# Attention into two feed-forward layers on one core: written order for the first two blocks, weight signs on ScalarE, integer sums on VectorE

## The chip, the cores and the metric

The kernel runs on one core of one Trainium2 chip. The metric is the device time of the program in microseconds (us). Five engines run side by side, each through its own queue of instructions in order: TensorE (PE in the profile; PEld is its weight load), VectorE (DVE), ScalarE (ACT), GpSimd (POOL) and SyncE (SP), which here only issues transfers. They meet at semaphores.

## What is computed

```python
q_d, k_d, v_d = means of q, k, v over groups of 4 positions   # 4 batches, 8 heads, 576 positions, width 64
out_up    = repeat(softmax(q_d k_d' / 8) v_d, 4)              # 144 pooled positions
out_local = softmax(q k' / 8, |i - j| < 4 only) v             # a band of 7 positions
x = (out_up + out_local) as 2304 x 512
y = (x w_a) * (x w_b) @ w_out                                 # 512 -> 1536 -> 512
h = y @ w_in                                                  # 512 -> 1024
s = h * softmax(h); s = (s - mean) / sqrt(var + 1e-6) * g
out = s @ w_out2                                              # 1024 -> 512
```

All inputs are 32-bit floats, except that the two layers' weights arrive as 64-bit floats, two 32-bit words each, and are made into 32-bit floats on the chip.

## The kernel before

The 2304 rows of x are cut into 18 tiles of 128 rows (s = 0 to 17), and two tiles make a block of 256 (0 to 8). Every matrix product on the long path is done three times in a reduced 32-bit format: the operand's high part by the weight's high part, the low part by the high, the high part by the low.

**Attention.** For each batch, `pooled_items` works on four pairs of heads (hp): VectorE sums q and k over 4 positions into `qkds` (L175), TensorE makes scores `S` (L196), VectorE their maximum (L206), ScalarE the exponentials `E` (L212), VectorE and GpSimd the normalisation (L218 to L221), TensorE turns `E` (`PT`, L232) and multiplies by the v that GpSimd has summed (`vds`, L184 and L185; `pv`, L244), and ScalarE writes `up`. `local_items` does the band for a tile s: scores `lS`, mask and maximum (L324 to L328), exponential, sum and normalisation (L335 to L338), turn (`lPT`), product with v (`lo`), the sum with `up` (L373) and the split into high and low part, `xTh` and `xTl` (L380, L381).

**Weights.** `w_stages` makes one 128 x 512 weight tile: transfer `raw` (L91), two ScalarE passes over the high and the low words (L99, L100), on VectorE a shift (L104) and the sign put back (L105), an integer sum of the two words on GpSimd (L110), the high part on ScalarE (L116) and the low part on VectorE (L123). There are 36 tiles for the first layer (three for each of 12 chunks j) and 16 for the second.

**First layer.** `emit_A` makes the two products of one block and one chunk (`ab`, 24 matmuls, L399) and multiplies them (L404 to L411); `emit_B` adds the third product (`acc` or `accS`, 12 matmuls, L426). A unit of A and B is called a step here; there are 108, and B comes two steps behind A. The list `subs` sets their order: three steps of block 0, then blocks 1 and 0 in turn, then one block after the other. A second phase (`emit_C`, `emit_chain`, `emit_D`) does the second layer, tile by tile.

**Order.** Attention and weight work is put on a list with places in units of half a step (`add(t, f)`) and called as the steps go by (`advance`). A scheduler then orders the instructions of each engine by its own timeline; before, `issue_after` held a few ScalarE instructions back in it (L82, L98).

Of the kernel before, what the change touches and what calls it, by code (L numbers as in the profile page):

```python
# [18 lines left out]
NP = H // 2  # L19
# [10 lines left out]
LEAD = 3  # L30
PT = [0, 16, 17]

# [6 lines left out]
def kernel(  # L39
# [17 lines left out]
    PE, ACT, DVE, POOL = nc.tensor, nc.scalar, nc.vector, nc.gpsimd  # L57
# [8 lines left out]
    mk_sb = base.tile([128, 4, KW], F32, name="mk_sb")  # L66
# [11 lines left out]
    gate = []  # L78

    def behind():  # L80

        return tc.issue_after(gate[-1].ins) if gate else nullcontext()  # L82

    def w_stages(src, i, dst, at, gcol=None, lo_eng=DVE):
# [4 lines left out]
        def load():  # L89
            raw = slot(at, I32, (128, 1024), "raw")  # L90
            nc.sync.dma_start(out=raw, in_=src[i])  # L91
            words = raw.rearrange("p (a b) -> p a b", b=2)
            st["low"], st["high"] = words[:, :, 0], words[:, :, 1]

        def s1():
            hw = f32(st["high"])
            prev = his.get((id(dst), i - 4))
            with behind(), (tc.issue_after(prev.ins) if prev else nullcontext()):  # L98
                ACT.activation(out=hw, in_=hw, func=AF.Copy, scale=2.0 ** -112)  # L99
                ACT.activation(out=st["low"], in_=st["low"].bitcast(U32), func=AF.Copy, scale=2.0 ** -29)  # L100

        def s2():
            st["w"] = base.tile([128, 512], I32, tag="wm", bufs=3, name="wm")
            DVE.tensor_scalar(out=st["w"], in0=st["high"], scalar1=3, scalar2=None, op0=ALU.logical_shift_left)  # L104
            DVE.scalar_tensor_tensor(  # L105
                out=st["w"], in0=st["high"], scalar=-(2 ** 31), in1=st["w"], op0=ALU.bitwise_and, op1=ALU.bitwise_or
            )

        def s3():
            POOL.tensor_tensor(out=st["w"], in0=st["w"], in1=st["low"], op=ALU.add)  # L110

        def s4():
            t = slot(at)
            dst[i] = t[:, 0, :], t[:, 1, :]
            if gcol is None:
                his[id(dst), i] = ACT.copy(out=dst[i][0], in_=f32(st["w"]))  # L116
            else:
                his[id(dst), i] = ACT.activation(out=dst[i][0], in_=f32(st["w"]), func=AF.Copy, scale=gcol)
# [12 lines left out]
    his = {}  # L131
# [20 lines left out]
    def load_qkr(i):  # L152
# [6 lines left out]
        for n in range(2):  # L159
            nc.sync.dma_start(out=qkr[i][n], in_=qkp[i, :, n, :])  # L160

    def load_v(i):
        t = slot(32 + i, F32, (128, 2, 512), "vp")[:72] if i < NP else pool_p.tile([72, 2, 512], F32, tag="vp", name="vp")
        nc.sync.dma_start(out=t, in_=vp[i])
        vr[i] = t

    def pooled_items(b, hp):
        i = b * NP + hp
        st = {}

# [17 lines left out]
        def scores():  # L188
            if b:
                st["S"] = [aps.tile([72, 2 * SD], F32, tag=f"x{e}", name="S") for e in range(2)]  # L190
            else:
                t = aps.tile([72, 2, 512], F32, tag="S", name="S")
                st["S"] = [t[:, e, 0:2 * SD] for e in range(2)]
            for half in range(2):
# [7 lines left out]
        def smax():  # L202
# [5 lines left out]
            st["E"] = pool_p.tile([72, 2, 2, SD], F32, tag="E", name="E")  # L208
# [31 lines left out]
        def pvm():  # L240
            st["pv"] = aps.tile([128, SD], F32, tag="x0", name="pv")
            for kh in range(2):
                for e in range(2):
                    PE.matmul(  # L244
                        out=st["pv"][e * 64:e * 64 + 64, :],
                        lhsT=st["v"][:, kh, e * 64:e * 64 + 64],
                        rhs=st["PTs"][:, e, kh, :], start=(kh == 0), stop=(kh == 1))
# [6 lines left out]
        items = [(0, qsum(0)), (0.5, qsum(1)), (1.5, scores), (2, vsum(0)), (2.2, vsum(1)),  # L254
                 (2.5, smax), (4.5, norm), (6, ptr), (7, pte), (8, pvm), (9, pve)]
        if b:
            items = [(-3, lambda: load_qkr(i)), (-2.9, lambda: load_v(i))] + items
        return items

    def load_local(s, st):  # L260
# [487 lines left out]
```

## Time and profile before

| | |
|---|---|
| median of 3 runs | 870.78 us (868.38 to 873.15) |
| profiled execution | 875.02 us, its span 871.6 us |
| TensorE busy | 803.8 us, 92% of the span |
| VectorE / ScalarE / GpSimd busy | 47% / 39% / 40% |
| mean granted TensorE clock | 0.988 of full speed |

The profile is of one execution. A row of a timeline gives the start, the duration, the engine, the line and the tiles (result <- operands), the number of instructions merged into it, and in brackets the idle time ahead of it and who ended it. A busy TensorE in such rows includes matmuls at its lower clock.

### The profile page before, as it was taken

The page shows a single profiled execution, that of the slowest core. Times are in us where ns is not written, and L with a number is a line of the kernel's source. Part 1 is how long each engine was busy: PE and PEld are TensorE (multiplying, and loading weights), DVE is VectorE, ACT ScalarE, POOL GpSimd, SP SyncE. Part 2 cuts the span into 40 slices and gives each one's busy share as a digit, 9 for nine tenths or more (in the row PEclk, how much of TensorE's full clock was granted, in tenths as well). Part 3 has the DMA queues.
Part 4 walks back from the last instruction along what each step waited for, and adds up shares of the span by engine and source line. Part 5 has one row for each costly group of instructions (what it writes and reads, how often), then busy time and mean ns, then how long its engine had stood idle before and what let it go on. Part 6 is the DMA issues. An engine that isn't in the chain of part 4 may idle for free. (4 is left out here: it accounts for less than half of the span.)

```text
span 871.6 us, 15806 instructions
## 1 busy us (share of the span) xinstructions
PE 803.8 (92%) x6456; PEld 731.6 (84%) x6456; DVE 411.8 (47%) x720; ACT 342.6 (39%) x768; POOL 351.3 (40%) x335
## 2 busy tenths in 40 slices
PE   2248898989999999999999999999989999999997
PEld 2137887979999999999999999999888888888886
DVE  4797689982223232223232221222894825555542
ACT  1654466752333333223332222323753534343432
POOL 2675576763133333223322222222883334333320
PEclk9999799999999999999999999999999999999999
DMA  7998300121212222112111110003730544444420
GB/s 203 339 300 316 116 14 29 42 66 53 82 49 77 66 66 66 53 41 73 44 40 40 49 39 15 25 8 102 258 101 25 157 145 141 142 142 145 132 73 36
DMA packets 65655, 85.21 MB, mean 98 GB/s; under 512 B 9368, under 2 KB 46552, under 8 KB 65584
## 3 DMA queue, kind: packets, MB, share of 16 engines
q1 hardware_dynamic: 55792, 79.49, 29.2%
q10 hardware_dynamic: 9792, 4.72, 1.9%
q8 instruction: 50, 0.82, 0.4%
q14 instruction: 21, 0.17, 0.1%
HBM read 66.89 MB, written 17.30 MB: 97 GB/s over the span
## 5 line engine op out<-in xcount | busy, mean ns | idle before, releaser
L399 PE MATMUL ab<-xTh,w 128*128 128x256 f32 x1728 | 348.0, 290 | 9.0 <-DVE a L407 7.5
L399 PEld LDWEIGHTS ab<-xTh,w 128*128 128x128 f32 x1728 | 282.9, 194 | 17.2 <-DVE a L407 9.2
L399 PE MATMUL ab<-xTl,w 128*128 128x256 f32 x864 | 247.2, 286 | 0.0
L411 POOL TENSOR_TENSOR pl<-a,ph 128x256 fp32r<-128x256 f32 x108 | 88.5, 820 | 210.0 <-ACT ph L410 210.0
L399 PEld LDWEIGHTS ab<-xTl,w 128*128 128x128 f32 x864 | 167.5, 194 | 1.0 <-issue 0.8
L407 DVE TENSOR_TENSOR a<-a,ab 128x256 f32<-128x256 f32 x108 | 45.0, 416 | 211.8 <-ACT a L404 211.7
L467 PE MATMUL h<-w,o1w 128*128 128x512 f32 x432 | 102.9, 391 | 1.3 <-DVE ss L491 1.3
L404 ACT COPY a<-ab 128x256 f32<-128x256 f32 x108 | 40.1, 371 | 157.2 <-PE ab L399 145.6
L426 PE MATMUL acc<-ph,w 128*128 128x256 f32 x480 | 98.4, 286 | 1.6 <-ACT ph L410 1.6
L110 POOL TENSOR_TENSOR wm<-wm,raw 128x512 int32<-128x512 int32 x52 | 79.9, 1542 | 40.9 <-DVE wm L105 22.1
L467 PEld LDWEIGHTS h<-w,o1w 128*128 128x128 f32 x432 | 80.5, 188 | 18.7 <-ACT o1w L455 1.7
L535 PE MATMUL o<-w,cTh 128*128 128x512 f32 x288 | 90.9, 397 | 0.9 <-ACT cTh L525 0.9
L426 PEld LDWEIGHTS acc<-ph,w 128*128 128x128 f32 x480 | 80.2, 194 | 2.5 <-ACT ph L410 1.8
L426 PE MATMUL accS<-ph,w 128*128 128x256 f32 x384 | 80.4, 290 | 0.0
L426 PE MATMUL acc<-pl,w 128*128 128x256 f32 x240 | 68.8, 288 | 0.5 <-POOL pl L411 0.5
L535 PEld LDWEIGHTS o<-w,cTh 128*128 128x128 f32 x288 | 54.1, 188 | 13.8 <-ACT cTh L525 1.1
L426 PEld LDWEIGHTS accS<-ph,w 128*128 128x128 f32 x384 | 64.8, 196 | 0.9 <-issue 0.6
L410 ACT CAST ph<-a 128x256 fp32r<-128x256 f32 x108 | 43.8, 405 | 38.1 <-DVE a L407 37.9
L535 PE MATMUL o<-w,cTl 128*128 128x512 f32 x144 | 57.2, 397 | 0.1
L519 POOL TENSOR_TENSOR cTl<-raw,cTh 128x1024 fp32r<-128x1024 f32 x15 | 36.0, 2402 | 50.4 <-ACT cTh L518 50.3
L426 PE MATMUL accS<-pl,w 128*128 128x256 f32 x192 | 55.4, 288 | 0.4 <-POOL pl L411 0.4
L105 DVE SCALAR_TENSOR_TENSOR wm<-raw,wm 128x512 int32<-128x512 int32 x52 | 50.9, 989 | 1.1
(84 smaller groups left out, 1118.8 us busy)
## 6 DMA issues: line engine op xcount, KB each, us to landing
raw<-w SPq DMA_DIRECT2D x52, 512.0 KB
qkr<-qkp SPq DMA_DIRECT2D x32, 288.0 KB
vd<-v SPq DMA_DIRECT2D x15, 512.0 KB
raw<-vd SPq DMA_DIRECT2D x60, 128.0 KB
vw<-vwin SPq DMA_DIRECT2D x36, 140.0 KB
vp<-vp SPq DMA_DIRECT2D x16, 288.0 KB
o1d<-o ACTq DMA_DIRECT2D x36, 128.0 KB
o1r<-o1d SPq DMA_DIRECT2D x18, 256.0 KB
```

Of the source, the lines that this page charges most:

```text
L105: DVE.scalar_tensor_tensor(out=st["w"], in0=st["high"], scalar=-(2 ** 31), in1=st["w"], op0=ALU.bitwise_and, op1=ALU.bitwise_or)
L110: POOL.tensor_tensor(out=st["w"], in0=st["w"], in1=st["low"], op=ALU.add)
L399: PE.matmul(out=ab[:, n, :], lhsT=w[:, ws], rhs=x[:, k, :], start=(k == 0 and i == 0), stop=(k == 3 and i == 2), skip_group_check=True)
L404: g_ = ACT.copy(out=a, in_=ab[:, 0, :])
L407: DVE.tensor_tensor(out=a, in0=a, in1=ab[:, 1, :], op=ALU.mult)
L410: ACT.copy(out=ph, in_=a)
L411: POOL.tensor_tensor(out=pl, in0=a, in1=f32(ph), op=ALU.subtract)
L426: PE.matmul(out=accs[blk][m // 2][:, m % 2, :], lhsT=w[:, ms], rhs=x, start=(j == 0 and i == 0 and m % 2 == 0), stop=(j == NCH - 1 and i = ...
L467: PE.matmul(out=h[:, n * 512:n * 512 + 512], lhsT=x[:, ks], rhs=w, start=(k == 0 and q_ == 0), stop=(k == 3 and q_ == 2))
L519: POOL.tensor_tensor(out=h4(lo), in0=raw, in1=f32(h4(hi)), op=ALU.subtract)
L535: PE.matmul(out=o, lhsT=x[:, k, :], rhs=w, start=(k == 0 and q_ == 0), stop=(k == 7 and q_ == 2))
```

## The change

- q and k of batch 0 are fetched first; mask and identity go to ScalarE's transfer queue, and an exponential of one column loads ScalarE's table at the start.
- For batch 0, v is no longer summed on GpSimd: TensorE multiplies by each of the four parts (16 matmuls for a pair of heads in place of 4).
- The sign is kept by a two-sided slope (`Prelu`) in the ScalarE pass over the high words, so L105 goes; the integer sum moves from GpSimd to VectorE.
- `LEAD` is 1: blocks 0 and 1 take turns from the first step, so all four tiles s = 0 to 3 are finished ahead of the first step.
- `pin` ties each instruction to the one written before it on its engine, for all that is written up to step 24; the early part has a new table of places. The three `issue_after` holds are gone.
- Twelve first-layer tiles (20 before) are fetched ahead; the buffer `o1` is single; scratch of the early part moves to slots of later weights (12 to 19).

```diff
-LEAD = 3
+LEAD = 1
+STRICT = 24
...
+    def pin():
+        traced = nc.cur_bb.bb.instructions
+        for ins in traced[done[0]:]:
+            if ins.engine in last:
+                tc.add_manual_dep(
+                    ins, last[ins.engine].name,
+                    mybir.DependencyInfo(mybir.DependencyClass.NoSync, mybir.DependencyReason.DATA), reason="pin")
+            last[ins.engine] = ins
...
-            with behind(), (tc.issue_after(prev.ins) if prev else nullcontext()):
-                ACT.activation(out=hw, in_=hw, func=AF.Copy, scale=2.0 ** -112)
+            ACT.activation(out=hw, in_=hw, func=AF.Prelu, scale=2.0 ** -112, alpha=2.0 ** 32)
...
-            DVE.scalar_tensor_tensor(
-                out=st["w"], in0=st["high"], scalar=-(2 ** 31), in1=st["w"], op0=ALU.bitwise_and, op1=ALU.bitwise_or
-            )
...
-            POOL.tensor_tensor(out=st["w"], in0=st["w"], in1=st["low"], op=ALU.add)
+            DVE.tensor_tensor(out=st["w"], in0=st["w"], in1=st["low"], op=ALU.add)
...
+                v = [vr[i][:, kh, 2 * D * t:2 * D * t + 2 * D] for kh in range(2) for t in range(4)]
...
+            if s < 4:
+                x = slot(16 + s, F32, (128, NP, 256), "lx")[:, :, 0:128]
...
-                o1 = base.tile([128, 2, 256], F32, tag="o1", bufs=2, name="o1")
+                o1 = base.tile([128, 2, 256], F32, tag="o1", name="o1")
...
+    for hp, ts in enumerate(((4.8, 5.5, 6.3, 7.6, 8.5, 10.7, 12, 13.9, 14.5, 18.4),
...
-        t = (-20, -14, -8)[j] + 0.8 * (i % 3) if j < LEAD else w_due[j] - 8 + 0.8 * (i % 3)
+        t = 4 * j - 6 + 1.33 * (i % 3)
...
+    ACT.dma_start(out=mk_sb[0:64, :], in_=band)
+    ACT.dma_start(out=mk_sb[64:128, 0:4], in_=band[:, 1:5])
+    ACT.dma_start(out=id_sb, in_=ident)
+    warm = base.tile([128, 1], F32, name="warm")
+    ACT.activation(out=warm, in_=mhalf, func=AF.Exp)
...
+        if u <= STRICT:
+            pin()
```

TensorE, the last attention work ahead of the first step, before: `ab` is the first step's tile, `lS` 16 times is a further tile's scores.

```order
L232 MATMUL PT<-id_sb,E 72x72 x8
L348 MATMUL lPT<-id_sb,lP 70x128 x4
L244 MATMUL pv<-PTs,vds 64x144 x4
L348 MATMUL lPT<-id_sb,lP 70x128 x8
L361 MATMUL lo<-lPTs,vw 64x64 x8
L348 MATMUL lPT<-id_sb,lP 70x128 x4
L361 MATMUL lo<-lPTs,vw 64x64 x24
L399 MATMUL ab<-xTh,w_485 128x256
L399 MATMUL ab<-xTh,w_512 128x256
L317 MATMUL lS<-qkr 64x70 x16
```

The same place now, from the last pair of heads' `pv` on.

```order
L269 MATMUL pv<-PTs,vp 64x144 x16
L394 MATMUL lo<-lPTs,vw 64x64 x16
L375 MATMUL lPT<-id_sb,lP 70x128 x8
L394 MATMUL lo<-lPTs,vw 64x64 x16
L375 MATMUL lPT<-id_sb,lP 70x128 x8
L394 MATMUL lo<-lPTs,vw 64x64 x16
L439 MATMUL ab<-xTh,w_508 128x256
L439 MATMUL ab<-xTl,w_508 128x256
```

Tiles 2 and 3 (the last two pairs of `lPT` and `lo`) now stand ahead of the first `ab`, and a `pv` has 16 matmuls.

SyncE's queue behind the first transfers, before: `raw` is a weight tile, `vw` the band's v; the last two rows are batch 1's first q, k and v.

```order
L91 DMA raw<-w 128x1024 x3
L271 DMA vw<-vwin 70x512 x4
L91 DMA raw<-w 128x1024 x18
L160 DMA qkr<-qkp 128x576 x2
L164 DMA vp<-vp 72x1024
```

The same place now; the seven `raw` of the third row are weight tiles 13 to 19.

```order
L100 DMA raw<-w 128x1024 x10
L703 DMA g_sb<-g 128x8
L100 DMA raw<-w 128x1024 x7
L606 DMA mk_sb<-band 64x70
L165 DMA qkr<-qkp 128x576 x2
L169 DMA vp<-vp 72x1024
```

Batch 1's q and k still stand behind the weights, and the last four of these weights (16 to 19) now go into slots that hold the sums `lx` of tiles 0 to 3.

VectorE where the first step's end meets the next weights, now (the second `qkds` rows are batch 1's, `w_674` and `w_703` are tiles 3 and 4).

```order
L410 TENSOR_TENSOR lx<-lo,up 128x4x128
L113 TENSOR_SCALAR wm<-raw 128x512
L116 ISA wm<-raw,wm 128x1024
L186 TENSOR_REDUCE qkds<-qkr 128x144
L113 TENSOR_SCALAR wm<-raw 128x512
L116 ISA wm<-raw,wm 128x1024
L186 TENSOR_REDUCE qkds<-qkr 128x144
L129 TENSOR_TENSOR w_674<-wm,w_674 128x512
L445 TENSOR_TENSOR a<-a,ab 128x256
L113 TENSOR_SCALAR wm<-raw 128x512
L116 ISA wm<-raw,wm 128x1024
L129 TENSOR_TENSOR w_703<-wm,w_703 128x512
```

The integer sum (L116) is there an instruction over 1024 elements, and the low parts of tiles 3 and 4 stand behind both sums of batch 1.

## Rows read from the trace of the kernel before

**Rows 1.** Busy time by stretch: five engines, granted clock, transfer share, GB/s.
```profile
0.00:75.90 75.90, 30.27 (x273) 21.08 (x273) 52.28 (x82) 34.25 (x86) 42.25 (x42) 1.00 0.88 278
75.90:234.10 158.20, 147.01 (x1267) 137.66 (x1268) 113.04 (x161) 80.02 (x190) 91.85 (x82) 0.95 0.23 75
234.10:600.00 365.90, 365.90 (x3573) 351.71 (x3572) 98.59 (x221) 107.72 (x287) 104.85 (x128) 1.00 0.17 49
```
**Rows 2.** Timeline, the end of the start: TensorE from 65 us on.
```profile
65.29 1.34 PE L244 MATMUL pv<-PTs,vds 72*64 72x144 f32 x8 [0.85 <-POOL vds L185]
66.56 1.92 PE L348 MATMUL lPT<-id_sb,lP 128*70 128x128 f32 x8
...
72.48 1.98 PE L361 MATMUL lo<-lPTs,vw 70*64 70x64 f32 x32 [0.86 <-DVE lx L373]
75.90 0.80 PE L399 MATMUL ab<-xTh,w 128*128 128x256 f32 x2 [1.44 <-ACT xTh L380]
```
**Rows 3.** One line, ScalarE L432: start of the first and the last.
```profile
L432 ACT COPY o<-accS x8: 566/588/592, 234.1 to 611.8; 128x512 f32<-128x512 f32 x8
```
**Rows 4.** TensorE's waits, 0 to 75.9 us: total, times, longest.
```profile
PE PT L232 <- POOL E L221: 17.2, 4, 5.4
PE lS L317 <- DMA qkr<-qkp: 12.3, 3, 8.9
```
**Rows 5.** Timeline, the first transfers and matmuls.
```profile
0.74 0.39 SPq L624 DMA_DIRECT2D id_sb<-ident  x1
...
4.95 3.75 SPq L160 DMA_DIRECT2D qkr<-qkp  x8
...
8.92 0.51 PE L317 MATMUL lS<-qkr 64*64 64x70 f32 x8 [8.92 <-DMA qkr<-qkp]
...
9.71 1.24 PE L196 MATMUL S<-qkds 64*72 64x144 f32 x8 [0.28 <-DVE qkds L175]
```
**Rows 6.** VectorE by line and shape, 0 to 234.1 us.
```profile
L123 DVE TENSOR_TENSOR w<-wm,w 128x512 fp32r<-128x512 f32 x36 | 43.6, 1227 | 4.5 <-ACT w L116 4.5
L105 DVE SCALAR_TENSOR_TENSOR wm<-raw,wm 128x512 int32<-128x512 int32 x36 | 35.1, 983 | 0.8
L104 DVE TENSOR_SCALAR wm<-raw 128x512 int32<-128x512 int32 x36 | 27.5, 770 | 6.8 <-ACT raw L99 6.5
L175 DVE TENSOR_REDUCE qkds<-qkr 128x144 f32<-128x576 f32 x18 | 12.7, 740 | 7.3 <-DMA qkr<-qkp 7.3
...
L373 DVE TENSOR_TENSOR lx<-lo,up 128x512 f32<-128x512 f32 x5 | 3.5, 690 | 3.5 <-PE lo L361 3.5
```
**Rows 7.** Timeline, VectorE and GpSimd on weights.
```profile
26.72 0.43 DVE L104 TENSOR_SCALAR wm<-raw 128x512 int32<-128x512 int32 x1 [4.91 <-ACT raw L99]
...
31.20 3.03 POOL L110 TENSOR_TENSOR wm<-wm,raw 128x512 int32<-128x512 int32 x2 [6.28 <-DVE wm L105]
31.59 1.50 DVE L104 TENSOR_SCALAR wm<-raw 128x512 int32<-128x512 int32 x1
...
34.91 0.68 DVE L105 SCALAR_TENSOR_TENSOR wm<-raw,wm 128x512 int32<-128x512 int32 x1
```
**Rows 8.** VectorE by line and shape, 640 us to the end.
```profile
L480 DVE SCALAR_TENSOR_TENSOR u<-h,u 128x1024 f32<-128x1024 f32 x18 | 22.1, 1225 | 36.1 <-ACT u L479 36.1
```
**Rows 9.** The chain that ended last: start, duration, what.
```profile
662.35 2.88 PE acc L426 x24
```
**Rows 10.** TensorE by line, 75.9 to 234.1 us: first and last of seven attention groups.
```profile
L196 PE MATMUL S<-qkds 64*72 64x144 f32 x32 | 6.7, 338 | 0.4 <-ACT up L252 0.4
...
L317 PE MATMUL lS<-qkr 64*64 64x70 f32 x32 | 1.2, 327 | 0.0
```
**Rows 11.** ScalarE by line and shape, 0 to 234.1 us.
```profile
L99 ACT ACTIVATE raw<-raw 128x512 f32<-128x512 f32 x36 | 24.4, 679 | 9.2 <-DMA raw<-w 9.2
...
L116 ACT CAST w<-wm 128x512 fp32r<-128x512 f32 x36 | 22.3, 620 | 33.6 <-POOL wm L110 33.5
```
**Rows 12.** TensorE's waits, 600 to 672 us.
```profile
PE ab L399 <- DVE a L407: 4.9, 3, 2.6
```

More of the change, by code (lines that the diff above doesn't have):

```diff
@@ L1 @@
-from contextlib import ExitStack, nullcontext
+from contextlib import ExitStack
 import concourse.bass as bass
@@ L241, in pvm @@
             st["pv"] = aps.tile([128, SD], F32, tag="x0", name="pv")
-            for kh in range(2):
+            if b:
+                v = [st["v"][:, kh] for kh in range(2)]
+            else:
+                v = [vr[i][:, kh, 2 * D * t:2 * D * t + 2 * D] for kh in range(2) for t in range(4)]
+            for n, vt in enumerate(v):
                 for e in range(2):
[L244 to L247, printed above, removed]
+                    PE.matmul(out=st["pv"][e * 64:e * 64 + 64, :], lhsT=vt[:, e * 64:e * 64 + 64],
+                              rhs=st["PTs"][:, e, n * 2 // len(v), :], start=(n == 0), stop=(n == len(v) - 1))
         def pve():
@@ L575 @@
-    first += [f for _, f in locs[1][1][:2]]
-    for a, b in zip(locs[0][1][2:], locs[1][1][2:]):
-        first += [a[1], b[1]]
-    for n, f in enumerate(first):
-        add(-50 + 0.1 * n, f)
-    for s, t0, ln in ((2, -6, 9), (3, -3, 9)):
-        for o, f in locs[s][1]:
-            add(t0 + o * ln / 12, f)
-    for b, t0, step, ln in ((1, 6, 6, 8), (2, 52, 9, 9), (3, 98, 9, 9)):
-        for hp in range(NP):
-            for o, f in pooled_items(b, hp):
-                add(t0 + step * hp + (o * ln / 9 if o >= 0 else o), f)
+    pool0 = [pooled_items(0, hp) for hp in range(NP)]
@@ new lines, in first @@
+    def first(*plan):
+        for t, items, name in plan:
+            add(t - 100, items[name])
+    add(-30, lambda: SP.dma_start(out=mk_sb[64:128, 4], in_=band[:, 0]))
+    for hp in range(NP):
+        add(-100 + 0.1 * hp, lambda hp=hp: load_qkr(hp))
+    for hp in range(NP):
+        add(-99 + 0.1 * hp, lambda hp=hp: load_v(hp))
+    for n, f in enumerate([wst[0][0], wst[1][0], locs[0]["loadv"], locs[1]["loadv"], wst[2][0], locs[2]["loadv"],
+                           locs[3]["loadv"]] + [wst[i][0] for i in range(3, 12)]):
+        add(-98 + 0.01 * n, f)
@@ new lines @@
+    names = ("qsum0", "qsum1", "scores", "smax", "exps", "norm", "ptr", "pte", "pvm", "pve")
+    for hp, ts in enumerate(((4.8, 5.5, 6.3, 7.6, 8.5, 10.7, 12, 13.9, 14.5, 18.4),
[3 rows of a table added]
+        first(*((t, pool0[hp], name) for t, name in zip(ts, names)))
+        first((4.8 + 1.5 * hp, locs[0], f"scores{hp}"))
+    first((14.8, locs[1], "scores"), (17.2, locs[2], "scores"), (18.6, locs[3], "scores"))
+    names = ("mask", "smax", "exps", "norm", "ptr0", "pte0", "ptr1", "pte1", "pvm0", "pvm1", "evac", "split")
@@ new lines @@
+    for s, ts in ((0, (13.1, 14.9, 17, 18.7, 20.9, 22.6, 21.2, 23.2, 24, 24.2, 26.8, 27.2)),
[3 rows of a table added]
+        first(*((t, locs[s], name) for t, name in zip(ts, names)))
+    for i, ts in enumerate(((18.7, 20.8, 20.9, 24.9, 25.9), (21.5, 22.6, 22.7, 27.6, 28.2),
+                            (28.3, 29, 29.1, 30.2, 31))):
+        for t, f in zip(ts, wst[i][1:]):
+            add(-100 + t, f)
+    offs = dict(load=-3, qsum0=0, qsum1=0.5, scores=1.5, vsum=2, smax=2.5, exps=2.6, norm=4.5, ptr=6, pte=7,
+                pvm=8, pve=9)
@@ new lines @@
+    early = dict(load=-6.9, qsum0=-2.2, qsum1=-1.8, scores=0, smax=0.6, exps=1.1, norm=2.1, vsum=0.5, ptr=8.1, pte=8.6, pvm=9.7,
+                 pve=10.3)
+    for b, t0, step in ((1, 2, 5.5), (2, 52, 9), (3, 98, 9)):
+        for hp in range(NP):
+            for name, f in pooled_items(b, hp).items():
+                add(t0 + step * hp + (early if b == 1 else offs)[name], f)
+    offs = dict(loadqk=-6, loadv=-5, scores=0, mask=1, smax=1.05, exps=1.1, norm=3, ptr0=5, pte0=5.1, ptr1=6, pte1=6.1, pvm0=7,
+                pvm1=8, evac=9, split=10)
@@ L587 @@
+    late = dict(loadqk=-6, loadv=-5, scores=0, mask=0.8, smax=0.85, exps=2, norm=3, ptr0=5.4, pte0=5.6, ptr1=5.8,
+                pte1=6.2, pvm0=7, pvm1=7.2, evac=8)
     for s in range(4, NSUB):
         t0 = 24 * (s // 2) - 20 + 8 * (s % 2)
-        for o, f in locs[s][1]:
-            add(t0 + (o * 9 / 12 if o >= 0 else o), f)
-    for i in range(3 * NCH):
+        for name, f in locs[s].items():
+            o = offs[name]
+            if s < 6:
+                add(46.1 if name == "split" else 29 + 8.4 * (s % 2) + late[name], f)
+            else:
+                add(t0 + (o * 9 / 12 if o >= 0 else o), f)
```

146 lines of the change are left out of this document (74 added, 72 removed), and 6 rows, old and new, of the table names.

## The prediction

> **What bounds the kernel now.** I read the busy time by stretch first [rows 1]. From 234.1 to 600 us TensorE is busy for all of 365.9 us at full granted clock: nothing done on the other engines can shorten that part. Ahead of it there are two stretches in which TensorE waits. Until 75.9 us it is busy 30.3 us of 75.9; at 75.9 the first step begins [rows 2]. From there to 234.1, where block 1's sums leave PSUM [rows 3], it is busy 147.0 of 158.2 at a mean granted clock of 0.95. A third, small one lies at 600 to 672, with 4.9 us of waits [rows 12]. So a change of the order and of the weight work can win in these three places only, and what it wins there reaches the end whole, since all that follows is TensorE's.
>
> Who holds TensorE up in the first stretch is read from its waits [rows 4]: 17.2 us for GpSimd's normalisation `E`, 12.3 us for q and k. GpSimd is late because 36 integer sums of 1.5 us each stand in its queue from 31 us on [rows 7]. VectorE is the next: 52.3 us busy of 75.9, then 113.0 of 158.2 [rows 1], and much of this is not work. A shift takes 0.43 us alone and 1.50 us beside a GpSimd sum [rows 7]; over 36 tiles it averages 0.77, the sign 0.98 against 0.68 alone, the low part 1.23 [rows 6], where the sum `lx`, an instruction of the same size, takes 0.69 [rows 6].
>
> **The start, part by part.** q and k are issued at 4.95 us behind seven small transfers that begin at 0.74, and the first pair's matmul runs at 8.92 [rows 5], 3.97 us after its issue. Issued at 0.74, it runs at 4.7: 4.2 us sooner.
>
> From there a round is q and k summed (two of 0.70, the run without contention; the mean is 0.74 [rows 6]), then scores 1.24 [rows 5], and `qkds` is one buffer, so rounds don't overlap: 2.8 us each. The fourth sum ends near 4.7 + 3 x 2.8 + 1.4 = 14.5, its scores near 16.
>
> Now the load. VectorE, counted in its new order up to the last `lx` of tile 3: eight sums of q and k (5.6), four maxima of pooled scores and their small operations (5), four bands of about 3.4 (mask, maximum, difference, sum: 13.6), three weights of 0.43 + 0.8 + 0.69 (5.8), four `lx` of 0.69 (2.8): 33 us. The three weights are where before it did eleven. TensorE gets more: `pv` had 4 matmuls (8 records) in 1.34 us [rows 2], with 16 it is at most four times that, 5.4, and at least two and a half times, 3.3, if most of a short group is latency; I take 4.2, in the middle. With `lPT` 1.92 and `lo` 1.98 a tile [rows 2], scores 1.24 and the turn of `E` about 1.2 a pair, band scores 1.3 a tile, this is 4 x (4.2 + 1.24 + 1.2 + 1.92 + 1.98 + 1.3) = 47 us in one queue, in a written order. It is the longest lane. Its first `pv` can start at 17.5 (exponentials and copy behind the fourth round's turn). I follow the order: pv 0, turn 1, band scores 1 and 2, pv 1, turn 2, band scores 3, half a `lPT`, pv 2, and so on, which gives pv 3 at 43 to 47. Then comes what hangs on it: `up`, `lx` of tiles 0 and 1, which stand on VectorE ahead of tile 3's mask, maximum and sum and a weight (about 8 us), GpSimd's 1.1, `lPT`, copies and `lo` (about 4). The first step starts near 58 us in place of 75.9: **-18**. The bounds: 46 if TensorE is not the lane (VectorE's 33 us behind 4.7 us, with 8 us of waits); 63 if each of GpSimd's eleven operations holds a VectorE instruction for half its length.
>
> What hides the rest: the table load is off the path and goes ahead of all; `Prelu` takes what the pass it replaces took, 0.68 [rows 11] (a table load for each change of function would add to it, but the new order has one load in all); GpSimd loses the sums of v of batch 0; mask and identity travel beside q and k on another queue and take a few tenths from them.
>
> **The integer sum on VectorE.** No row shows it. It reads and writes the two tiles of the sign operation that goes, 0.68 us undisturbed [rows 7]; in the order it is an instruction over 1024 elements, and the nearest such row takes 1.23 [rows 8]. I take 0.8, near the lower end, since the bytes and the strided operand are those of the first row. Either way VectorE pays for one instruction less or about the same, while GpSimd loses 36 x 1.51 = 54 us in the first 234 us.
>
> [...]
>
> **The two first blocks.** 24 matmuls take 2.88 us [rows 9], a step of 36 therefore 4.32, 24 steps 103.7, and two A parts that run ahead of the end 5.8. The attention work of this stretch is 27.9 us in seven groups [rows 10]; tiles 2 and 3, about 6 us of it, now lie ahead of the first step: 22. That makes 131.5 us of TensorE work; before, 137.4 and 158.2 in fact. Before, 11.2 us were idle [rows 1] and about 8 went to the granted clock of 0.95 [rows 1].
>
> Now a new wait. SyncE's queue holds batch 1's first q and k behind weight tiles 16 to 19, and tile 19 waits for tile 3's split: `lx`, `xTh` 0.6, `xTl` 1.4, then issue and transfer as at the start, 4 to 5 us with those weights ahead. VectorE stands at that sum with the low parts of weight tiles 3 and 4 behind it, and TensorE, in the middle of its second step, at batch 1's scores. Two steps (5.8 us) cover part of some 9; I count 4 lost. In the rest VectorE has 33 x 1.92 + 26 x 0.41 + about 20 of attention = 94 us in 142, ScalarE the work it had; 6.5 us for the stalls of engines that may no longer pass a late instruction, and for the clock behind pauses. The stretch takes 142 in place of 158.2: **-16**. Bounds: 133 to 158.
>
> **The second layer's weights.** 4.9 us of waiting are for `a` on VectorE [rows 12], where 16 weight tiles crowd between 600 and 660. With no sums on GpSimd beside them: **-4.4**; bounds 0 and -7. The single `o1` makes ScalarE wait for a transfer nine times, some 2 us each; two `ab` buffers cover that, 0; uncovered it is 18 us.
>
> **Sum.** -18 - 16 - 4.4 = -38.4 against the profiled execution's 875.0: 836.6. The median of the runs is 4.2 lower, which gives **832**.
>
> **Rivals.** *The order is better than I count.* If TensorE's long `pv` overlaps what I put behind it, the first step starts at 46 (-30) and the blocks lose 6 in place of 10.5 (-20.5), with -5 later: 875 - 55.5 - 4 = 815. For it: VectorE's lane alone would allow it; against: each written order waits at its worst place.
>
> *VectorE becomes the bound.* At 1.22 a sum, 94 becomes 108 of 142, and each GpSimd operation (some 55 in the stretch, 0.8 to 1.4 long) may still hold one of VectorE's. Start 61, blocks 152, nothing won at 600: -15 - 6 - 0, 875 - 21 - 4 = 850. For it: 0.43 to 1.50 beside GpSimd [rows 7]. Against: GpSimd has half of the work left.
>
> *The written order loses the overlap: slower.* If no ScalarE pass of the next weight runs while VectorE adds and subtracts, a weight is a chain of two passes of 0.68, a shift of 0.43, the sum 0.8, the cast 0.62 and the low part 0.69 [rows 6, 7, 11], 3.9; three are 11.7, the two `a` chains of a pair of steps 2.4, its share of batch 1's attention 3: 17 us for a pair of steps, against 8.6 + 2 of TensorE. Twelve pairs at 6.4 lost are 77: start 58, blocks 208, +32, 903. It decides the sign from a loss of about 3 us a pair (18 + 21.5 of slack over twelve). Against: the order puts the next weight's two passes ahead of the cast.
>
> *The change doesn't do what it says*: the start is a matter of bytes (278 GB/s over 75.9 us [rows 1]), and q and k are hidden anyway. Then only the blocks win, about 850 too. Against: the first 6 MB are enough for the first step; I put it with the second rival.
>
> **Chances.** Forecast 0.47 (820 to 842), better 0.22, VectorE or bytes 0.24, slower 0.04, and 0.03 for a loss that just eats the gain. Measured differences of under 0.5% (4 us) can't be told from none. Faster 0.93, the same 0.03, slower 0.04. The range, 808 to 853, holds forecast and the two rivals beside it and leaves out their tails.
>
> **What would show it.** First `ab` at 46 to 63 us in place of 75.9; weight sums of 0.7 to 1.2 on VectorE; TensorE's wait for `qkds` in the second step; block 1's last sums leaving near 200 us; no wait for `a` at 620 to 650; from 234 on the same rhythm, earlier. Wrong: a first `ab` above 65, a loss of over 2 us a pair in the blocks, or a second table load.

## The result and the profile after

The changed kernel took 834.90 us, the median of four runs (833.01 to 841.63), beside 870.12 us for the kernel before in the same comparison (868.38 to 873.15): a ratio of 0.9606, 95% interval 0.9545 to 0.9666. The forecast was 832.

The profiled execution took 833.01 us, its span 831.2. Busy time by stretch, cut at the first step (53.86) and where block 1's sums leave (203.0); the columns are those of [rows 1]:

```profile
0.00:53.86 53.86, 37.21 (x481) 30.32 (x481) 33.52 (x69) 24.86 (x70) 13.39 (x15) 0.88 0.84 272
53.86:203.00 149.14, 133.04 (x1158) 127.75 (x1157) 98.39 (x173) 89.30 (x206) 50.16 (x57) 0.95 0.39 123
203.00:831.20 628.20, 623.59 (x4918) 571.10 (x4916) 232.82 (x478) 228.38 (x493) 191.06 (x196) 1.00 0.27 83
```

The last of them before the change, which no group shows:

```profile
234.10:871.60 637.50, 626.53 (x4920) 572.84 (x4918) 246.45 (x478) 228.31 (x493) 217.24 (x212) 1.00 0.27 82
```

| stretch | predicted | measured |
|---|---|---|
| to the first step | 75.9 to 58: -18 | 53.86: -22.0 |
| to block 1's last sums | 158.2 to 142: -16 | 149.14: -9.1 |
| from there to the end | -4.4 | 637.5 to 628.2: -9.3 |
| span | -38.4 | -40.4 |

The sum came out; its terms for the start and for the two first blocks did not. Block 1's sums leave at 203.0 in place of 234.1 [rows 3]:

```profile
L470 ACT COPY o<-accS x8: 572/587/587, 203.0 to 586.6; 128x512 f32<-128x512 f32 x8
```

TensorE in the start, a timeline as in [rows 2]:

```profile
5.32 0.51 PE L339 MATMUL lS<-qkr 64*64 64x70 f32 x8 [5.32 <-DMA qkr<-qkp]
...
18.75 4.40 PE L269 MATMUL pv<-PTs,vp 72*64 72x144 f32 x32 [1.47 <-ACT PTs L258]
...
26.26 2.44 PE L269 MATMUL pv<-PTs,vp 72*64 72x144 f32 x32
...
37.32 2.13 PE L269 MATMUL pv<-PTs,vp 72*64 72x144 f32 x32
40.57 1.98 PE L394 MATMUL lo<-lPTs,vw 70*64 70x64 f32 x32 [1.12 <-DVE lx L410]
...
51.95 1.98 PE L394 MATMUL lo<-lPTs,vw 70*64 70x64 f32 x32
```

The same 16 matmuls take 4.40 us at 18.75 and 2.13 at 37.32: TensorE went from a lower level of its clock to an upper one at about 26 us. From 42 us on it is back at the lower one: the granted clock reads 0.50, and 16 records of `lo` take 1.12 us at 45.59 in place of 0.69 at 35.19 (stretch, TensorE's busy time, granted clock, transfers):

```profile
20.00:24.00 4.00, 4.00 (x34) 1.00 0.92 241
...
42.00:44.00 2.00, 2.00 (x20) 0.50 0.53 203
```

The forecast counted the whole start at the lower level.

TensorE's waits between 53 and 200 us (total, times, longest):

```profile
PE S L209 <- DVE qkds L186: 7.2, 2, 3.8
PE lPT L375 <- POOL lP L365: 3.7, 2, 2.5
PE pv L269 <- ACT PTs L258: 3.1, 2, 1.7
PE PT L252 <- ACT E L232: 1.8, 3, 1.3
```

The longest single one, 3.8 us at 60 to 64, is the predicted wait for batch 1's q and k. The weight work on VectorE until 200 us, beside [rows 6, 7]:

```profile
L116 DVE CUSTOM_DVE_ANT_0 wm<-raw,wm 128x1024 uint16<-128x1024 uint16 x36 | 28.5, 791 | 3.6 <-ACT raw L109 0.2
L129 DVE TENSOR_TENSOR w<-wm,w 128x512 fp32r<-128x512 f32 x36 | 28.5, 790 | 2.3 <-ACT w L122 2.1
L113 DVE TENSOR_SCALAR wm<-raw 128x512 int32<-128x512 int32 x36 | 23.4, 649 | 13.1 <-ACT raw L108 13.1
```

The sum takes 0.79 us on average. The low part fell from 1.23 to 0.79, the shift from 0.77 to 0.65.

### The profile page after: what moved, and what is told of

Same layout as the page of the kernel before. It is cut to its first block, busy times and chain, and to the rows that moved or that the text cites. A ratio compares the mean times of both kernels' runs of the same rounds, so it can differ in the third digit from the quotient of the medians.

```text
span 831.2 us, 15927 instructions
## 1 busy us (share of the span) xinstructions
PE 793.8 (96%) x6552; PEld 729.2 (88%) x6552; DVE 364.7 (44%) x720; ACT 342.5 (41%) x769; POOL 254.6 (31%) x267
## 4 chain that ended last, share of the span: by engine, by line
PE 84%; DVE 7%; ACT 5%; DMA 2%; issue 1%; POOL 1%; SPq 0%; DVEq 0%; ACTq 0%; POOLq 0%
PE ab L439 33%; PE o L573 12%; PE h L505 12%; PE acc L464 9%; PE accS L464 7%; PE lo L394 3%; PE lPT L375 2%; PE pv L269 2%; PE lS L339 2%; DVE wm L116 1%; DVE w L129 1%; DMA qkr<-qkp 1%; PE S L209 1%; DVE wm L113 1%; ACT raw L108 1%
## 5 line engine op out<-in xcount | busy, mean ns | idle before, releaser
L449 POOL TENSOR_TENSOR pl<-a,ph 128x256 fp32r<-128x256 f32 x108 | 84.8, 785 | 261.1 <-ACT ph L448 261.0
L444 ACT COPY a<-ab 128x256 f32<-128x256 f32 x108 | 40.1, 371 | 154.6 <-PE ab L439 149.6
L464 PE MATMUL acc<-ph,w 128*128 128x256 f32 x480 | 96.5, 283 | 0.0
L464 PE MATMUL accS<-ph,w 128*128 128x256 f32 x384 | 78.2, 285 | 0.0
L464 PEld LDWEIGHTS acc<-pl,w 128*128 128x128 f32 x240 | 46.0, 192 | 0.1
L514 DVE TENSOR_REDUCE mx<-h 128x1 f32<-128x1024 f32 x18 | 22.0, 1224 | 51.6 <-PE h L505 51.6
```

The source lines that it names most:

```text
L444: ACT.copy(out=a, in_=ab[:, 0, :])
L449: POOL.tensor_tensor(out=pl, in0=a, in1=f32(ph), op=ALU.subtract)
L464: PE.matmul(out=accs[blk][m // 2][:, m % 2, :], lhsT=w[:, ms], rhs=x, start=(j == 0 and i == 0 and m % 2 == 0), stop=(j == NCH - 1 and i = ...
L514: DVE.tensor_reduce(out=mx, in_=st["h"], axis=AX.X, op=ALU.max)
```

## The experiments

Two kernels take parts of the change alone into the kernel before (E5, E11), one adds the early fetch to that (E12); the others alter the changed kernel. "Before" beside them is 871 to 873 us.

**E1: batch 1's q, k and v earlier.**

```diff
+                if (b, hp, name) == (1, 0, "load"):
+                    add(-97.87, f)
+                    continue
```

> The changed kernel with one difference: batch 1's first q, k and v are issued after weight tile 8, ahead of weight tiles 9 to 19, and not behind them. Theory (the wait for `qkds` in the second step is that queue and nothing else): the first 3.8 us wait of TensorE goes, and the matmuls at the lower clock behind it (64 to 68 us) go with it, another 1.5 to 2 us; the first step stays within 1 us of 53.9; block 1's last sums leave at 197 to 199 in place of 203.0, and the time falls by 4 to 6 us, to 827 to 829. Rival (VectorE is the bound in the blocks, and a wait that goes comes back as another): the first wait goes, but waits further on grow by as much, block 1's sums leave within 1.5 us of 203.0 and the time is within 2 us of 833.

Measured: 833.21 us, but in two groups: 828.72, 828.77, 829.09 and 837.34, 837.59, 837.80. The profiled run is of the three near 837.5:

```profile
17.94 4.40 PE L269 MATMUL pv<-PTs,vp 72*64 72x144 f32 x32 [1.49 <-ACT PTs L258]
...
25.45 4.11 PE L269 MATMUL pv<-PTs,vp 72*64 72x144 f32 x32
...
32.73 4.11 PE L269 MATMUL pv<-PTs,vp 72*64 72x144 f32 x32
...
38.52 0.69 PE L252 MATMUL PT<-id_sb,E 72*72 72x72 f32 x4 [0.19 <-ACT lPTs L383]
...
42.96 4.05 PE L269 MATMUL pv<-PTs,vp 72*64 72x144 f32 x32
```

Here no `pv` of the start runs at the upper level, and the first step comes at 61.4. The changed kernel's times fall in the same way, 833.01 to 835.73 and, in a single run, 841.63. Only one execution of each kernel was profiled; the other runs are told apart by their mean granted clock, in which a start at the lower level throughout counts as 1.00 (E1's profile reads 1.00 over its 61.4 us): 0.981 to 0.986 near 829 and 0.991 to 0.995 near 837.5 here, 0.979 to 0.984 and 0.990 for the changed kernel. Group against group the gain is 5.4 and 4.1 us, as the theory said. In the profile the first wait for `qkds` is gone, the second has grown from 3.4 to 4.4, and the blocks' stretch takes 145.9 in place of 149.1.

**E2: v of batch 0 summed on GpSimd, 4 matmuls for a `pv`.**

```diff
-                v = [vr[i][:, kh, 2 * D * t:2 * D * t + 2 * D] for kh in range(2) for t in range(4)]
+            v = [st["v"][:, kh] for kh in range(2)]
...
+        first((4.8 + 1.5 * hp, locs[0], f"scores{hp}"), ((7, 9, 11, 14)[hp], pool0[hp], "vsum"))
```

> The changed kernel with one difference: for batch 0 v is again summed on GpSimd ahead of each pair's normalisation, into scratch beside `E` (no buffer is shared between pairs), and a `pv` has 4 matmuls in place of 16. Theory of the prediction (TensorE is the longest lane of the start, 4 us of it for each `pv`): `pv` falls from 2.1 to 4.4 us each to about 0.7 to 1.3, the lane loses 8 us, GpSimd's 16 added operations (0.6 to 1.0 us each, 13 us in all) lie in its free time, and the first step starts 3 to 8 us sooner, at 46 to 51; time 825 to 830. Rival (GpSimd's queue decides, as it did before the change): the normalisations `E` come 2 to 4 us later each, TensorE waits for `PT` again, the first step starts at 56 to 62, and the time is 835 to 841.

Measured: 833.98 us (832.31 to 836.09), one group, first step at 53.5.

```profile
18.29 1.18 PE L253 MATMUL PT<-id_sb,E 72*72 72x72 f32 x8 [5.57 <-POOL E L242]
...
25.00 1.23 PE L266 MATMUL pv<-PTs,E 72*64 72x144 f32 x8
```

Neither range holds it, and both mechanisms are there. At the same lower level (16 records of `lo` take 1.12 us in both) the first step is 7.9 us sooner than E1's 61.4, so the 16 matmuls are a real lane; and TensorE waits 5.57 us for the first `E` in place of 0.57, since GpSimd's sums stand ahead of that normalisation.

**E3: no written order.** `if u < 0: pin()`.

> The changed kernel without the tie of each instruction to the one written before it: the scheduler's own order on every engine, all else as it is. Theory A (the written order is most of what the start won): VectorE does the shifts, sums and low parts of some nine more weight tiles (1.9 us each, 17 us) ahead of the first `lx`, the first step starts at 62 to 72 in place of 53.9; in the blocks about half of that is given back, since those weights are then done; time 840 to 850. Theory B (the weight work and the early q and k won it, the order nothing): first step within 3 us of 54, time within 3 us of 833, or a little less, since no instruction then waits in a written place (16 us of waits between 54 and 203).

Measured: 849.88 us (846.45 to 852.12), first step at 73.0.

```profile
0.00:73.00 73.00, 44.03 (x424) 34.62 (x424) 53.07 (x106) 51.64 (x121) 14.36 (x17) 1.00 0.97 304
73.00:222.60 149.60, 141.52 (x1234) 134.04 (x1238) 66.54 (x136) 62.65 (x157) 55.75 (x55) 0.95 0.23 73
```

Theory A: VectorE works 53.1 us ahead of the first step in place of 33.5 and ScalarE 51.6 in place of 24.9, on weights that nobody needs yet (15 tiles finished in place of 3). The 15 us between the medians are not all the order's: this start ran at the lower level (`pv` 4.1 to 4.4), and beside the changed kernel's one run of that kind, 841.63, three of the four runs (849.65 to 852.12) are 8 to 10 us later.

**E4: E3 with the sum on GpSimd.**

> As the kernel without the written order, and besides the integer sum back on GpSimd (the sign stays in the ScalarE pass). To be read against that kernel. Theory (GpSimd's sums slow VectorE and hold up GpSimd's own attention work): a sum takes 1.4 to 1.5 us on GpSimd; VectorE's shift rises from 0.65 to 0.75 or more and the low part from 0.79 to 1.0 or more between the start and the end of block 1; the normalisations on GpSimd come later; time 4 to 15 us above the kernel without the written order. Rival (VectorE's own load is what counts): VectorE loses 36 sums of 0.79 us, 28 us by block 1's end, and the time is the same or up to 8 us less.

Measured: 859.80 us (858.05 to 861.76), 9.9 more than E3; first step at 72.8, the blocks' stretch 155.4 (E3: 149.6), from there on 631.3 (627.7). The theory, not the rival: VectorE has 36 sums fewer and yet works 128.4 us until block 1's sums leave in place of 119.6, since its shift averages 0.82 us in place of 0.51 and its low part 1.19 in place of 0.72.

**E5: the weight work alone, in the kernel before.**

```diff
-                ACT.activation(out=hw, in_=hw, func=AF.Copy, scale=2.0 ** -112)
+                ACT.activation(out=hw, in_=hw, func=AF.Prelu, scale=2.0 ** -112, alpha=2.0 ** 32)
...
-            DVE.scalar_tensor_tensor(
-                out=st["w"], in0=st["high"], scalar=-(2 ** 31), in1=st["w"], op0=ALU.bitwise_and, op1=ALU.bitwise_or
-            )
...
-            POOL.tensor_tensor(out=st["w"], in0=st["w"], in1=st["low"], op=ALU.add)
+            DVE.tensor_tensor(out=st["w"], in0=st["w"], in1=st["low"], op=ALU.add)
```

> The kernel before with the weight work of the change alone: the sign in the ScalarE pass, the integer sum on VectorE; order, loads and buffers are those of before. Theory (the sums on GpSimd cost what the two kernels without written order differ by, and the start is a matter of order): about 10 us, of which 3 to 5 in the second layer's weights (no 4.9 us of waits for `a`), 5 to 6 in the two first blocks, about none ahead of the first step; time 858 to 864. Rival (the start of before was held up by GpSimd's queue, 17.2 us of waits for `E`): the first step comes 8 to 14 us sooner, at 62 to 68 in place of 75.9, and the time is 846 to 855.

Measured: 838.60 us (836.94 to 844.27), ratio 0.9639 (0.9598 to 0.9680).

```profile
0.00:68.20 68.20, 28.35 (x272) 20.01 (x272) 39.89 (x82) 33.52 (x86) 23.30 (x31) 0.99 0.92 289
68.20:206.60 138.40, 137.16 (x1266) 130.75 (x1267) 86.61 (x161) 78.52 (x190) 50.47 (x57) 0.98 0.30 96
206.60:836.50 629.90, 624.53 (x4920) 571.39 (x4918) 234.07 (x478) 228.43 (x493) 192.14 (x196) 1.00 0.27 83
```

Both expectations fell: I had taken the price from E3 and E4, in which the sign was already gone. The weight work alone brings 32.7 us; the whole change brought 35.2. It wins in all three stretches (-7.7, -19.8, -7.6), and in the blocks TensorE is busy 137.2 of 138.4 us at a mean granted clock of 0.98, better than in the changed kernel (133.0 of 149.1, 0.95).

**E6: q and k behind seven small transfers again.**

> The changed kernel with one part undone: the identity, the masks and the row g go on SyncE's queue ahead of q and k, seven small transfers as before. Theory of the prediction (q and k are worth 4.2 us): the first pair's matmul starts at 9 to 9.6 in place of 5.3, and the whole start moves with it by 3.5 to 4.5 us, time 837 to 840 where TensorE keeps its pace. Rival (the fetch is hidden: the bytes of weights and v and VectorE's lane set the first step): the first matmul moves by about 4 us, the first step by less than 1.5 us, time within 2 us of the changed kernel's.

Measured: 839.96 us, in two groups: 835.39 and 836.33, 843.60 and 844.15. The profiled run is the last, with the whole start at the lower level as in E1's:

```profile
8.69 0.51 PE L339 MATMUL lS<-qkr 64*64 64x70 f32 x8 [8.69 <-DMA qkr<-qkp]
```

The first matmul is 3.4 us later than the changed kernel's, the first step (64.6) 3.2 later than E1's, the times of a group some 1.5 to 2.5 us above the changed kernel's. The fetch counts: 3.2 us at the first step, and about half the term of 4.2 in the time.

**E7: E1 with TensorE kept busy until 18 us.** 25 matmuls on zeros in the gaps.

```diff
+                PE.matmul(out=o[:, 0:128], lhsT=zz[0][:, 0:128], rhs=zz[0][:, 128:256], start=True, stop=True,
...
+    for t, n in ((4.7, 14), (6.25, 4), (9.25, 3), (11.9, 1), (14.4, 3)):
+        add(t - 100, spin(n))
```

> The kernel with batch 1's q, k and v fetched earlier (828.72 to 837.80 in six runs, three near 829 and three near 837.5), with one more thing: 25 matmuls of 128 x 128 on zeros, into a PSUM buffer that nobody reads, before the first q and k and in TensorE's four waits until 18 us, so that TensorE is hardly idle from 1 to 18 us. In the profile of the changed kernel the three later `pv` took 2.44, 2.18 and 2.13 us, in that of the kernel with the earlier fetch 4.11, 4.11 and 4.05: two levels of the clock for the same instructions. Theory (an execution has the one or the other, and what TensorE did ahead of it decides): with TensorE kept busy the upper level comes in every run and earlier, the first `pv` takes 2.2 and not 4.4, the first step starts at 50 to 55 us, and all runs lie at 825 to 831 with a spread of under 3 us. Rival (which level comes is a matter of the execution, not of what TensorE did): the two groups of times stay, some 9 us apart.

Measured: 830.81 us; the runs 826.54, 829.36, 830.49, 831.12, 837.18, 838.09. The profiled run (826.54), first step at 50.3:

```profile
17.11 3.19 PE L269 MATMUL pv<-PTs,vp 72*64 72x144 f32 x32
23.41 2.91 PE L269 MATMUL pv<-PTs,vp 72*64 72x144 f32 x32
28.56 2.18 PE L269 MATMUL pv<-PTs,vp 72*64 72x144 f32 x32
```

In this run the upper level is there before the first `pv` (scores `S` 0.71 us in place of 1.24), goes within it and comes back by the third (granted clock 1.00 until 18 us, 0.50 from 20 to 24, 1.00 from 26 to 28), yet the runs still spread over 11.6 us. The theory fell as to the spread and the first `pv` (3.19, not 2.2). The mean granted clock of all six is 0.961 to 0.981, lowest in the two slowest.

**E8: E1 and E2 together, each pair's sums behind its normalisation.**

```diff
+        first((4.8 + 1.5 * hp, locs[0], f"scores{hp}"), (ts[5] + 0.05, pool0[hp], "vsum"))
```

> Both at once: batch 1's q, k and v fetched earlier, and v of batch 0 summed on GpSimd with 4 matmuls for a `pv`, each pair's sums now behind its normalisation and not ahead of it. Theory (the sums cost TensorE's wait of 5.6 us for the first `E` only by their place): that wait goes, the first step starts at 50.5 to 52.5, TensorE at the lower level throughout, the first wait for `qkds` goes too, and the time is 825 to 829 in one group of runs. Rival (the start is set by VectorE's lane and by GpSimd's place at the end of it, TensorE has slack now): the first step stays within 1 us of 53.5, time 828 to 831.

Measured: 828.24 us (826.78 to 829.02), one group, ratio 0.9505 (0.9479 to 0.9531): the lowest median of this study.

```profile
13.94 1.18 PE L253 MATMUL PT<-id_sb,E 72*72 72x72 f32 x8 [1.13 <-POOL E L242]
...
17.23 1.47 PE L266 MATMUL pv<-PTs,E 72*64 72x144 f32 x8 [0.95 <-ACT PTs L259]
```

First step at 51.5, the whole start at the lower level (`lo` 1.12 as in E1), blocks 146.4. The theory, in each of its numbers.

**E9: E8 with the written order for the start alone.** `STRICT = 0`.

> The kernel with both (batch 1's q, k and v earlier, v summed on GpSimd behind the normalisation; 826.78 to 829.02), with the written order kept only for what is written ahead of the first step; from there the scheduler orders each engine, with the same loads and the same turn of blocks. Theory (in the blocks the written order costs: TensorE waited 16 us between 54 and 203 in the changed kernel for instructions that may not be passed, but 2 us where the weight work alone was changed, a stretch of 138.4 in place of 149.1): the first step stays at 50 to 52 or comes a little sooner, block 1's last sums leave at 186 to 192 in place of 197.9, time 817 to 823. Rival (the waits are those of blocks that take turns from the first step, with weights made as they are used, whoever orders them): the stretch stays within 2 us of 146, time 826 to 830; or the scheduler pulls weights ahead of the last `lx` as in the kernel without any written order, first step at 60 or later, time above 832.

Measured: 840.21 us (838.16 to 841.92). TensorE's waits until 60 us, the longest group:

```profile
PE lPT L372 <- ACT PTs L259: 13.1, 2, 11.7
```

The theory fell. The order of the start ties only the instructions written before the first step; the scheduler put weight passes between them, 13 ahead of the first step in place of E8's 3. One of these stood in ScalarE's queue for a transfer that had not landed, with the copy `PTs` behind it, and that is most of the long wait:

```profile
33.96 0.65 ACT L108 ACTIVATE raw<-raw 128x512 f32<-128x512 f32 x1 [11.07 <-DMA raw<-w]
```

The first step comes at 55.8, 4.3 us later than E8's, and the blocks' stretch takes 155.4, 9.0 more (it holds some of the start's work: 1238 matmul records in place of 1158); behind them 1.2 are won. With these loads and turns the written order beyond the start is worth 12 us.

**E10: E8 with places moved.** Sums, turns, products and copies of batch 1, and likewise turns, products and copies of the band's tiles 4 and 5.

```diff
-    early = dict(load=-6.9, qsum0=-2.2, qsum1=-1.8, scores=0, smax=0.6, exps=1.1, norm=2.1, vsum=0.5, ptr=8.1, pte=8.6, pvm=9.7,
-                 pve=10.3)
+    early = dict(load=-6.9, qsum0=-3.7, qsum1=-3.3, scores=0, smax=0.6, exps=1.1, norm=2.1, vsum=0.5, ptr=8.6, pte=9.1, pvm=10.2,
+                 pve=10.8)
```

> The same kernel as the one with both, with the written order kept through step 24 and eight of its places moved: batch 1's sums of q and k 1.5 units (half steps) sooner, turn, copy, product and copy of a pooled pair 0.5 later, turn and product of the band's tiles 4 and 5 some 0.6 later. Theory (TensorE waits in single written places; a place moved behind its operand is a wait less): the first step unchanged (51.5), the 4.4 us wait for `qkds` falls to under 1, the waits for `PTs`, `E` and `lP` (7.4 us in all) by half; block 1's last sums leave at 190 to 193, time 819 to 823. Rival (VectorE and ScalarE are full in this stretch, and what is put ahead holds up something else): waits for `qkds` go and waits for `a`, `w` or `E` come, time 826 to 830.

Measured: 832.63 us (828.71 to 834.82). Waits from 50 us to 215:

```profile
PE PT L253 <- ACT E L233: 3.1, 4, 2.3
PE lo L391 <- ACT lPTs L380: 2.5, 2, 1.5
PE pv L266 <- ACT PTs L259: 2.4, 2, 2.1
PE acc L461 <- POOL pl L446: 1.9, 2, 1.0
...
PE S L210 <- DVE qkds L186: 0.2, 1, 0.2
```

The rival's mechanism: the 4.4 us for `qkds` are nearly gone, and waits for `lPTs` and `pl` have come; the stretch takes 147.1 (146.4), the first step is the same (51.6). But the profiled run is the one of 828.71, with a mean granted clock of 0.975; the other three, 832.62 to 834.82 at 0.991 to 0.994, were not profiled, and where their 4 us beside E8 went is not shown.

**E11: the sign alone, in the kernel before** (E5 with the sum left on GpSimd).

> The kernel before with one half of the weight work: the sign in the ScalarE pass (VectorE's operation goes, 0.98 us on average), the integer sum still on GpSimd. The whole weight work brought 33 us (838.6 beside 871.3). Theory (most of it is GpSimd's sum, which holds up GpSimd's own attention work and slows what VectorE does beside it): the sign alone brings 6 to 12 us, time 859 to 865; the first step at 73 to 76, and TensorE's waits for `E` ahead of it stay at 13 us or more. Rival (VectorE's load is the bound, and 52 operations fewer on it, 45 us, are what counts): the sign alone brings 20 us or more, time 851 or less, and the sum on VectorE is about neutral for it.

Measured: 847.22 us (845.24 to 850.78), ratio 0.9720 (0.9682 to 0.9757).

```profile
0.00:69.60 69.60, 30.41 (x273) 21.45 (x273) 45.13 (x71) 33.78 (x86) 38.59 (x42) 1.00 0.92 295
69.60:209.60 140.00, 137.58 (x1266) 130.30 (x1267) 85.37 (x135) 79.57 (x189) 85.43 (x82) 1.00 0.27 89
```

Its low part and shift on VectorE until 215 us, and TensorE's wait for `E` until 75:

```profile
L120 DVE TENSOR_TENSOR w<-wm,w 128x512 fp32r<-128x512 f32 x36 | 45.7, 1280 | 11.7 <-ACT w L113 10.8
L104 DVE TENSOR_SCALAR wm<-raw 128x512 int32<-128x512 int32 x36 | 26.6, 744 | 7.5 <-ACT raw L99 6.9
```

```profile
PE PT L229 <- POOL E L218: 10.9, 4, 5.1
```

The rival: one VectorE operation fewer a tile brings 25.8 us, with GpSimd's 36 sums still there and shift and low part as slow as before. Of the 18.2 us won in the blocks 8.8 are waits (11.2 before, 2.4 here) and 9.4 are TensorE's own: nearly the same matmuls (1266 records, 1267 before) keep it busy 137.6 us in place of 147.0 at a mean granted clock of 0.95. Moving the sum brings about 7 more (32.7 in E5), so it isn't neutral: by the two profiled spans 8.7, of which 5.7 lie behind block 1, where E11 takes 635.6 us and E5 629.9.

**E12: E5 with q and k first.**

```diff
-    nc.sync.dma_start(out=id_sb, in_=ident)
+    ACT.dma_start(out=id_sb, in_=ident)
```

and the masks likewise.

> The kernel before with the weight work of the change (838.6 by itself) and q and k fetched first: the identity and the masks that are needed early go on ScalarE's queue, the rest behind the weights; no written order, and the blocks' turn as before. Theory (q and k are worth what the changed kernel with seven transfers ahead of them lost, 1.5 to 3.5 us): the first matmul at 5 to 5.5 us, the first step 2 to 4 us sooner than 68.2, time 834.5 to 837, which is the changed kernel's: then the written order, the turn from the first step and v by 16 matmuls bring nothing together. Rival (GpSimd's sums of v and normalisations set the first step there): the first step within 1 us of 68, time 837.5 to 840.

Measured: 839.71 us (839.32 to 843.17). The first step comes 2.6 us sooner (65.6), and the blocks take it back (141.9 beside 138.4). The time is the rival's, the first step nearly the theory's. Here a first step that comes sooner was worth nothing in the time; that what feeds the next steps did not come sooner too is the likely reason, and no run shows it.

## Why the prediction was right, and where it was not

**The time.** Right by its sum: errors of its terms offset one another, and that is luck. Some 7.5 us of the start are the upper level of the clock (E1's first step at 61.4 less 53.86, an estimate), which the forecast did not count on; the one run without it, 841.63, is nearly 10 us above 832. The mechanism in the large, less work and fewer stalls on the engines that feed TensorE in its first 234 us, is the one that the runs show; which part of the change wins it was read wrongly (below).

**The start (-18; -22.0).** The bounds held. Three of its terms were off. (1) The `pv` at 4.2 us is right at the lower level (4.05 to 4.40), and in the profiled run three of four ran at the upper one (2.13 to 2.44). In E1's run without it the first step is at 61.4: at the level that I counted with, the start is worth about -14.5, and 58 was 3 us short. (2) q and k: 5.32, not 4.7, and worth 3.2 us at the first step (E6), not 4.2. (3) GpSimd's sums of v I costed as work it is glad to lose; E2 and E8 show that 4 matmuls and the sums in the right place are the better bargain: 51.5 at the lower level. "It is the longest lane", of TensorE, was right: with 4 matmuls for a `pv` the first step comes 7.9 (E2) and 9.9 us (E8) sooner at the same level.

**The two first blocks (-16; -9.1).** This is the step that was mis-sized, in both of its terms. The 131.5 was work at the upper level; of the 133.0 that TensorE was busy, the mean granted clock of 0.95 over 149.1 us took some 7 (an estimate, worked out like the prediction's 8 for the stretch before), which leaves about 126. The attention work there is 16.1 us in six groups, not 22; two of them:

```profile
L209 PE MATMUL S<-qkds 64*72 64x144 f32 x32 | 2.9, 298 | 7.2 <-DVE qkds L186 7.2
L394 PE MATMUL lo<-lPTs,vw 70*64 70x64 f32 x66 | 2.6, 228 | 0.0
```

The loss, 4 for batch 1's q and k and 6.5 for other stalls and the clock, was 16.1 of waits and those 7, about 23 in place of 10.5. The named wait was 3.81 long against 4 (E1 removes it); a second wait for `qkds` behind it, 3.4, `lPT` 3.7, `pv` 3.1 and `PT` 1.8 make up the rest of the waits. In E10, the one attempt to move them, other waits came in their place.

**Where the gain comes from.** The prediction read GpSimd's `E` as what held the start, and set the removed sign against the added sum: "Either way VectorE pays for one instruction less or about the same, while GpSimd loses 36 x 1.51 = 54 us". The runs weigh it the other way round: the sign going from VectorE is worth 25.8 us by itself (E11), with TensorE still waiting 10.9 us for `E`, and the sum leaving GpSimd about 7 more in the order of before, 9.9 in the new kernel without the written order (E4). The row that pointed there was among the first that I read: VectorE 113.0 of 158.2 us [rows 1]. Cut into slices of 10 us it is busy 68 of the 70 us from 116 to 186, and 2 of the 10 from 196 (the columns of [rows 1]):

```profile
126.00:136.00 10.00, 9.57 (x80) 9.37 (x79) 9.93 (x12) 6.93 (x21) 6.85 (x6) 1.00 0.17 61
...
166.00:176.00 10.00, 9.63 (x74) 8.39 (x74) 9.90 (x12) 4.59 (x11) 7.17 (x7) 1.00 0.06 15
...
196.00:206.00 10.00, 10.00 (x119) 9.72 (x117) 2.00 (x5) 2.62 (x6) 3.52 (x6) 1.00 0.22 61
```

and two of TensorE's waits there were for it:

```profile
PE PT L232 <- DVE lP L324: 3.5, 1, 3.5
...
PE ab L399 <- DVE a L407: 2.6, 4, 1.1
```

In E11, with 85.4 us of VectorE in the blocks, the first of them is gone and the second is 0.4. Everything else, the early fetch, the written order, the turn from the first step and the 16 matmuls, adds up to about 4 us (838.60 in E5 to 834.90), which the intervals of the two ratios do not tell from none, by the two profiled spans 5.3: -14.3 to the first step, half of it by the level of the clock in that run, +10.7 in the blocks and -1.7 behind them. The changed kernel's one run without the upper level, 841.63, is no faster than E5 (836.94 to 844.27), whose profiled start has a mean granted clock of 0.99 (the changed kernel's 0.88). In the new arrangement the written order is needed: without it the kernel takes 849.88 (E3).

**The integer sum (0.8).** Measured 0.791 on average until 200 us; over all 52 the median is 0.69 and the least 0.69, the time of `lx` with its 512 elements of 32 bits (0.69 [rows 6]). The rival by which VectorE becomes the bound did not come: no run shows its 1.22 for the sum (0.79 on average here, 0.76 in E5), which is the time of another operation over 1024 elements (1225 ns [rows 8]).

**The second layer's weights (-4.4; -9.3 for all that follows block 1).** The waits for `a` [rows 12] are gone; 1.3 us for `ss` went too, and TensorE is busy 2.9 us less, of which some 1.8 are the granted clock, 0.97 behind those waits before and 1.00 now (an estimate from the two rows). Sixty microseconds there before,

```profile
640.00:700.00 60.00, 55.69 (x323) 49.07 (x323) 41.92 (x70) 29.36 (x53) 28.59 (x23) 0.97 0.31 92
```

and after:

```profile
615.00:675.00 60.00, 60.00 (x312) 51.16 (x311) 28.23 (x60) 24.18 (x41) 18.85 (x17) 1.00 0.34 105
```

From block 1 to the end TensorE idles 4.6 us in place of 11.0. The term was read from one wait and left out the other and the clock behind them.

**The rest.** `o1` held ScalarE up 15.6 us in eight waits, and an `a` 1.0 of them: the cover held. `Prelu` took 0.68, and there is one table load (1.28 us). The rival by which the order loses 6 us a pair of steps did not come; 16.1 us of waits over twelve pairs are 1.3 a pair, 1.9 with the clock, just below the 2 that would have shown the prediction wrong.

**Open.** What decides whether TensorE reaches the upper level during the start isn't settled: the same program has both. Whether the sum on GpSimd costs the same within the written order wasn't tried. Taking the sign off VectorE shortens both VectorE's work and the chain of each weight tile; no run takes these two apart. What the 16 matmuls and the turn from the first step are worth by themselves in the kernel before wasn't tried either.

## What to carry to other kernels

An engine at 71% of a stretch can be full for much of it: read its busy time in slices, take an operation off it first, and test that alone before an order is written around it. A term that is read from a wait has the clock behind the wait in it as well (0.97 behind the waits for `a` here, 1.00 without them). Where a written order holds an engine in single places, moving a place may only choose the next wait.

## What the runs showed of the hardware

- In the start nearly the same instructions ran at either level of TensorE's clock, and by the mean granted clocks one and the same program does (0.979 to 0.984 and 0.990, the changed kernel). Where it stays at the lower level (`pv` 4.05 to 4.40 us, E1's profiled run), TensorE is busy without a gap from 17.9 to 38.3 us and doesn't rise; in the changed kernel it rose at about 26 us (`pv` 4.40 before, 2.44 to 2.13 from there), after 7.5 us without a gap. The two groups of times are 7 to 9 us apart (the changed kernel, E1, E6).
- The granted clock reads 1.00 until the first fall that the trace records, also while matmuls run at the lower level: `pv` 4.40 and 2.13 us both stand in stretches with 1.00 (changed kernel, 18.75 and 37.32 us). Early on the level is read from durations.
- VectorE's operations were longer with the sums on GpSimd: there the low part averages 1.28 us and the shift 0.74 (E11), with the sums on VectorE 0.85 and 0.46 (E5). In the changed kernel the shortest sum on VectorE takes 0.69, and one of 52 took 2.08.
